# A convolution and a gated feed-forward layer on one core: the second stream's x issued first, the reciprocals' diagonal in two operations, a first weight slice of 256 columns, and shared casts

## The chip, the cores and the metric

The kernel runs on one core of a Trainium2 chip. The time is the device time of one execution in microseconds. The engines named below are TensorE (PE; its weight loads are PEld), VectorE (DVE), ScalarE (ACT), GpSimd (POOL) and SyncE (SP). DMA transfers are issued from the queues of SP and GpSimd; a transfer that converts from 32 to 16 bits is issued from GpSimd here.

## What is computed

x is (8, 4096, 192) in float32: 8 batches, 4096 positions, 192 channels in 8 heads of 24. A causal convolution over 7 positions has one set of 7 weights for each head, after a softmax over the 7. Its result, taken as 32768 tokens of 192, goes through a layer with a gate.

```
w = exp(weight - max(weight));  w = w / (sum(w) + 1e-9)        # (8, 7)
a[b, s, h, :] = sum over k of w[h, k] * x_pad[b, s + k, h, :]    # 6 zeros ahead of each batch
out = (relu(a @ w_gate) * (a @ w_val)) @ w_out                  # 192 -> 1536 -> 192
```

## The kernel before

**Streams and units.** The 8 batches are two streams of 4 (`st` 0 and 1). A unit is 1024 tokens of each stream, 16 units in all; a window is 512 tokens, two to a unit. The gate and value matmuls have only 64 rows to contract at a time (three chunks `c` of 64 channels), so the two streams lie on partitions 0 to 63 and 64 to 127 and run beside each other in the two halves of the array. That is why the gate and value weights `Wg` and `Wv` lie twice in SBUF: each slice of columns is loaded to partitions 0 to 63 by DMA (`load_w`, converting) and then copied to partitions 64 to 127 (`both_halves`; `pool_halves` does it on GpSimd for both weights).

**One unit.** `gate_val` (L528) goes through 12 slices `f` of 128 of the 1536 hidden channels. For each it makes the gate and the value product of both streams in two PSUM tiles (L541), then ACT applies the relu (`gr`, L552) and VectorE multiplies by the value product into `hT` (L553). There are four PSUM tiles of two banks, used in turn, so slice f+2 reuses the tiles of slice f. `project` multiplies `hT` by `Wo` (L570), and the result is copied and stored. The convolution of later units is done beside this on VectorE, ACT and GpSimd ("lanes"), from a transposed copy of x.

**The opening.** The first unit can't wait for the lanes, so its convolution runs on TensorE, as banded matrices. `first_block` (L388) makes the first window: for each chunk `c`, `conv_dense` (L352) multiplies pieces of x by the bands, 40 matmuls (L377) a chunk, and the result is evicted to `xc` (L392). In chunk 0 all pieces 1 to 4 of stream 0 come first, then those of stream 1, then piece 0 of both. `second_block` does the second window ahead of slice f=5.

The x of the first block comes in three transfers: stream 0, pieces 1 to 4, on SP in float32 into a staging area (`stage`, L104, in the room of the tile `prods`; issue L122), from where ACT casts it in two parts of the channels (L317); stream 1, pieces 1 to 4, on GpSimd, converted on the way (L127); piece 0 of both streams on SP into the staging area (L138), behind a clearing of its first rows (L137), cast by VectorE (L335).

**The bands.** `weight` lands in `wr`. VectorE takes the maximum (L251), ACT the exponentials into `ex`, 16 copies of each (L254); the row KW of `ex` holds 1e-9. VectorE sums (L258), takes the reciprocal (L259), and lays it on a diagonal of 8x8, `over` (L261), from the mask `spaced`, which GpSimd clears (L126) and fills with a diagonal (`affine_select`, L128). From the mask VectorE also makes `same` and `places` (L238). PE spreads the normalised weights over partitions (L272); VectorE makes `diag` (L282); 14 small matmuls (L292) place them as bands in PSUM; the bands are cast to 16 bits, heads 0 to 2 and 3 on VectorE, 4 to 7 on ACT (L329). The taps for the lanes are scaled on ACT (L304) and copied over partitions by DMAs on SP (L310). Between these steps PE runs matmuls on constants whose results nobody reads (`warm_up`, L154): 6 of 512 columns and one of 256 ahead of the spread matmul, 512 behind it, and 512 behind L292.

**Order.** The kernel is written with a manual schedule: each engine does its instructions in the order of the program, and waits are set from the data. GpSimd's order in the opening is: clear `spaced`, stream 1's x, the mask, weight slices 0, 1, 2 (each gate, then value), the x of the second block, slice 3, `pool_halves(2)`, slice 4, the gate half of slice 5, `pool_halves(3)`, the value half of slice 5. The slices' borders (`CUTS`, L165) are 0, 128, 384, 640, 896, 1152, 1536. VectorE copies slice 0 to the upper half while chunk 0 is computed (L358), and slice 1 after the first block and ahead of the first `hT` product (L659). After that come `pool_halves(4)`, `Wo`, `pool_halves(5)` and the first lane on GpSimd.

## Time and profile before

| | us |
|---|---|
| median of 3 runs | 765.97 (765.93 to 766.0) |
| profiled execution, span from first to last instruction | 764.4 |
| around the span (median less span) | 1.6 |
| PE busy | 760.3 (99%) |
| VectorE busy | 705.6 (92%) |
| ACT busy | 600.9 (79%) |
| GpSimd busy | 378.4 (50%) |
| first gate matmul (L541) on the chain | 7.72 |

The profiled execution has no time of its own beside its span, so it is set against the median of the runs. Times on a timeline count from the first instruction. PE's matmuls are pipelined: one of 512 columns is shown with 0.376 us, while the next pair starts after 0.216 us. A line such as L154 is a line of the kernel before; the changed kernel has other numbers for the same lines. The idle time in brackets is put down to what came last before the instruction started.

### The profile page before, as it was taken

To read this page: it belongs to the slowest core of one execution; us is meant where nothing else is said; L and a number is where in the kernel's file an instruction comes from. 1 tells how busy PE (TensorE), PEld (TensorE's weight loads), DVE (VectorE), ACT (ScalarE), POOL (GpSimd) and SP (SyncE) were. 2 spreads that over 40 slices of the span, in tenths; PEclk is the share of its full clock that TensorE was granted. 3 is DMA by queue.
4 is the path that set the end of the run, shared out by engine and by line. 5 is a ranking of instruction groups with operands and counts; after the bars stand their busy time and mean duration, and the time that the engine had idled before them with its cause. 6 is when DMAs were issued, how large, how long until landed. Compare 5 with 4: busy or idle time off the path is not lost.

```text
span 764.4 us, 25103 instructions
## 1 busy us (share of the span) xinstructions
PE 760.3 (99%) x10929; PEld 501.3 (66%) x10929; DVE 705.6 (92%) x763; ACT 600.9 (79%) x735; POOL 378.4 (50%) x244
## 2 busy tenths in 40 slices
PE   9999999999999999999999999999999999999998
PEld 5494674947649476584855848567494674947648
DVE  7998999999999999999999999999999999999891
ACT  6787887878878887887878878787787887876571
POOL 9419448093571926729175390853909347090000
PEclk9999999999999999999999999999999999999999
DMA  9969039290452805528073271722819134220202
GB/s 123 134 102 148 7 96 81 65 111 22 95 67 83 97 23 107 49 85 94 30 112 40 85 94 44 120 16 90 89 44 125 13 97 60 66 48 15 71 1 84
DMA packets 131830, 56.00 MB, mean 73 GB/s; under 512 B 96392, under 2 KB 131720, under 8 KB 131720
## 3 DMA queue, kind: packets, MB, share of 16 engines
q1 hardware_dynamic: 90680, 38.81, 23.9%
q0 software_dynamic: 40896, 15.50, 20.3%
q8 instruction: 85, 1.39, 0.8%
q14 instruction: 25, 0.20, 0.1%
q10 hardware_dynamic: 144, 0.10, 0.0%
HBM read 31.48 MB, written 25.17 MB: 74 GB/s over the span
## 4 chain that ended last, share of the span: by engine, by line
PE 99%; DVE 0%; ACT 0%; issue 0%
PE ps L541 65%; PE ps L570 32%; PE ps L619 1%; PE ps L377 0%; PE ps L154 0%; PE ps L411 0%; DVE band L329 0%; PE ps L272 0%; ACT acc L596 0%; PE ps L292 0%
## 5 line engine op out<-in xcount | busy, mean ns | idle before, releaser
L553 DVE TENSOR_TENSOR hT<-gr,ps 128x1024 f16<-128x1024 f16 (+1 forms) x386 | 469.0, 1216 | 36.6 <-ACT gr L552 9.4
L552 ACT ACTIVATE gr<-ps 128x1024 f16<-128x1024 f32 (+1 forms) x386 | 392.9, 1019 | 101.9 <-PE ps L541 99.7
L491 POOL TENSOR_TENSOR prods<-prods 128x1344 f32<-128x1344 f32 x70 | 212.4, 3034 | 290.0 <-DVE prods L487 286.7
L541 PE MATMUL ps<-xc,Wg 64*128 64x512 f16 x2304 | 311.9, 376 | 0.0
L541 PE MATMUL ps<-xc,Wv 64*128 64x512 f16 x2304 | 311.9, 376 | 0.0
L570 PEld LDWEIGHTS <-hT 64*128 64x128 f16 x5952 | 245.9, 94 | 3.7
L570 PE MATMUL ps<-Wo,hT 64*128 64x192 f16 x5952 | 248.1, 243 | 0.0
L541 PEld LDWEIGHTS <-Wv 64*128 64x128 f16 x2304 | 129.8, 94 | 118.5 <-DVE hT L553 0.3
L541 PEld LDWEIGHTS <-Wg 64*128 64x128 f16 x2304 | 112.3, 94 | 132.8 <-issue 0.2
L515 DVE SCALAR_TENSOR_TENSOR acc<-x_r,tap,acc 128x576 f32<-128x576 f16 x225 | 165.3, 813 | 0.0
L485 ACT ACTIVATE prods<-x_r,tap 128x448 f32<-128x448 f16 x222 | 130.1, 660 | 0.0
L596 ACT COPY out_s<-ps 128x768 f32<-128x768 f32 (+1 forms) x64 | 45.5, 711 | 51.3 <-PE ps L570 40.0
L203 POOL DMA_DIRECT2D x_e<-in_x_dram x58 | 47.0, 823 | 16.6 <-ACT acc L501 12.8
L465 POOL COPY x_p<-x_e 128x960 f16<-128x960 f16 (+1 forms) x58 | 50.3, 906 | 1.2 <-DMA x_e<-in_x_dram 1.1
L491 POOL TENSOR_TENSOR xc<-prods 128x1344 f16<-128x1344 f32 x14 | 42.4, 3029 | 1.1
L515 DVE SCALAR_TENSOR_TENSOR xc<-x_r,tap,acc 128x576 f16<-128x576 f16 x45 | 34.1, 813 | 0.0
L501 ACT ACTIVATE acc<-x_r,tap 128x576 f32<-128x576 f16 x45 | 31.4, 763 | 0.0
L487 DVE TENSOR_SCALAR prods<-x_r,tap 128x448 f32<-128x448 f16 x70 | 26.6, 450 | 0.0
L596 DVE COPY out_s<-ps 128x384 f32<-128x384 f32 (+1 forms) x16 | 8.7, 541 | 11.9 <-PE ps L619 9.4
L619 PE MATMUL ps<-Wo,hT 128*128 128x192 f16 x96 | 8.1, 246 | 0.0
L619 PEld LDWEIGHTS <-hT 128*128 128x128 f16 x96 | 7.9, 98 | 0.2 <-issue 0.2
L154 PE MATMUL ps<-const-bfloat16-1.0 128*128 128x512 bf16 (+1 forms) x9 | 3.9, 572 | 0.8 <-PEq L719 0.8
(54 smaller groups left out, 56.3 us busy)
## 6 DMA issues: line engine op xcount, KB each, us to landing
out_dram<-out_s SPq DMA_DIRECT2D x62, 384.0 KB, 2.7
x_e<-in_x_dram POOLq DMA_DIRECT2D x34, 192.0 KB, 7.4
x_e<-in_x_dram POOLq DMA_DIRECT2D x24, 240.0 KB, 5.6
x_r<-x_p SPq DMA_TRANSPOSE x131, 5.1
Wo<-in_moe_w_out_dram POOLq DMA_DIRECT2D x1, 576.0 KB, 7.3
x_h<-in_x_dram POOLq DMA_DIRECT2D x2, 210.0 KB, 4.8
Wg<-in_moe_w_gate_dram POOLq DMA_DIRECT2D x4, 96.0 KB, 4.1
Wv<-in_moe_w_val_dram POOLq DMA_DIRECT2D x4, 96.0 KB, 4.0
```

What stands on the lines that cost most here:

```text
L203: first = nc.gpsimd.dma_start(out=xe[:, j0 + start : j0 + n, st, :, :].rearrange("p j c r -> p j (c r)"), in_=bass.AP(tensor=x.tensor, off ...
L465: nc.gpsimd.tensor_copy(out=xp[:, j0 : j0 + n, :, st, :], in_=xe[:, j0 : j0 + n, st, :, :])
L485: engine.activation(out=out, in_=in_, func=ACTF.Copy, scale=scale)
L487: engine.tensor_scalar(out=out, in0=in_, scalar1=scale, scalar2=None, op0=ALU.mult)
L491: nc.gpsimd.tensor_tensor(out=pr[:, 0] if k < KW - 1 else xc[v + 1][:, :, LDVE:UNIT], in0=pr[:, 0], in1=pr[:, k], op=ALU.add,)
L501: nc.scalar.activation(out=accs[v][:, c, :], in_=shifted(v, c, 0, 0), func=ACTF.Copy, scale=tap[:, c, 0:1],)
L515: nc.vector.scalar_tensor_tensor(out=xc[v][:, c, 0:LDVE] if k == KW - 1 else acc[:, c, :], in0=shifted(v, c, k, 0), scalar=tap[:, c, k : k ...
L541: nc.tensor.matmul(out=pss[i][:, st, :], lhsT=W[64 * st : 64 * st + 64, c, 128 * f : 128 * (f + 1)], rhs=xcb[64 * st : 64 * st + 64, c, WI ...
L552: nc.scalar.activation(out=gr[:, sts], in_=pss[0][:, sts], func=ACTF.Relu)
L553: nc.vector.tensor_tensor(out=h[:, f, sts], in0=gr[:, sts], in1=pss[1][:, sts], op=ALU.mult)
L570: mm = nc.tensor.matmul(out=outs[q], lhsT=h[64 * r : 64 * r + 64, f, st, 128 * q : 128 * (q + 1)], rhs=Wo[64 * r : 64 * r + 64, f, :], sta ...
L596: one(out=dst[:, step * j : step * j + step], in_=src[:, step * j : step * j + step])
```

## The change

Seven places change, all in the opening:

- GpSimd issues stream 1's x ahead of the clearing of `spaced` and of the mask.
- The staging area's first rows are cleared by GpSimd, behind the mask, instead of VectorE.
- The first warm-up is 5 of 512 and one of 384 columns; the last one 512 and 256.
- The weight slices have 256 columns each. Slice 0 now covers f=0 and f=1. VectorE copies its first 128 columns to the upper half during chunk 0, and the other 128 after the first block, ahead of slice 1.
- Slice 1's gate and value loads are two calls, and between them GpSimd casts part of stream 0's x: pieces 3 and 4, channels 64 and up. ACT casts the first 64 channels of all pieces, and of pieces 1 and 2 the rest.
- The diagonal `over` is made without `sm`: a row of `ex` gets 2^127 off the diagonal and 0 on it, the sum over the rows is taken for each column, and its reciprocal is 1/sum on the diagonal and next to 0 off it. `sm` and the taps are made later, on VectorE, ahead of the band casts.
- In the first block VectorE evicts chunk 2 instead of chunk 1.

```diff
     nc.sync.dma_start(out=stage(0, SUB, 0, 1, 1, GSUB - 1), in_=body(0))
+    nc.gpsimd.dma_start(out=xts[0][0:SUB, 1:GSUB, 1, :], in_=body(1))
     ones = const.tile([128, SUB], FP)
...
     nc.gpsimd.memset(spaced[:], 0.0)
-    nc.gpsimd.dma_start(out=xts[0][0:SUB, 1:GSUB, 1, :], in_=body(1))
     nc.gpsimd.affine_select(
...
-    nc.vector.memset(stage(0, 32, 0, 2, 0, 1), 0.0)
+    nc.gpsimd.memset(stage(0, 32, 0, 2, 0, 1), 0.0)
...
-    warm_up(512, 512, 512, 512, 512, 512, 256)
+    warm_up(512, 512, 512, 512, 512, 384)
...
-    CUTS = [0, 128, 384, 640, 896, 1152, DFF]
+    CUTS = [0, 256, 512, 768, 1024, 1280, DFF]
...
-    def both_halves(copy, s, dst):
-        cols = slice(CUTS[s], CUTS[s + 1])
+    def both_halves(copy, s, dst, half=None):
+        lo, hi = CUTS[s], CUTS[s + 1]
+        cols = slice(lo, hi) if half is None else slice(lo + 128 * half, lo + 128 * half + 128)
         copy(out=dst[64:128, :, cols], in_=dst[0:64, :, cols])
...
+    def cast_x(copy, j0, j1, cols):
+        copy(
+            out=xts[0][0:ROWS0, j0:j1, 0, cols],
+            in_=stage(0, ROWS0, 0, 1, j0, j1 - j0)[:, :, cols],
+        )
+
     load_w(0)
-    load_w(1)
+    load_w(1, 1)
+    cast_x(nc.gpsimd.tensor_copy, 3, 5, slice(64, D))
+    load_w(1, 2)
     load_w(2)
...
+    FAR = 2.0**127
+    nc.vector.tensor_scalar(
+        out=ex[:, KW + 1, 0:H],
+        in0=spaced[0:H, 0, GAP : GAP + H],
+        scalar1=-FAR,
+        scalar2=FAR,
+        op0=ALU.mult,
+        op1=ALU.add,
+    )
...
-    nc.vector.tensor_reduce(out=sm[:], in_=ex[:, :, 0], axis=mybir.AxisListType.X, op=ALU.add)
-    nc.vector.reciprocal(sm[:], sm[:])
     over = const.tile([H, H], FP)
-    nc.vector.tensor_scalar(
+    nc.vector.tensor_reduce(
         out=over[:],
-        in0=spaced[0:H, 0, GAP : GAP + H],
-        scalar1=sm[:],
-        scalar2=None,
-        op0=ALU.mult,
-    )
+        in_=ex[:, :, 0:H].rearrange("h k j -> h j k"),
+        axis=mybir.AxisListType.X,
+        op=ALU.add,
+    )
+    nc.vector.reciprocal(over[:], over[:])
...
-    warm_up(512)
+    warm_up(512, 256)
 
     taps = const.tile([H, KW], FP)
-    nc.scalar.activation(taps[:], ex[:, 0:KW, 0], ACTF.Copy, scale=sm[:])
+    sm = const.tile([H, 1], FP)
+    nc.vector.tensor_reduce(
+        out=sm[:], in_=ex[:, 0 : KW + 1, 0], axis=mybir.AxisListType.X, op=ALU.add
+    )
+    nc.vector.reciprocal(sm[:], sm[:])
+    nc.vector.tensor_scalar(
+        out=taps[:], in0=ex[:, 0:KW, 0], scalar1=sm[:], scalar2=None, op0=ALU.mult
+    )
...
-    for cols in (slice(0, 64), slice(64, D)):
-        nc.scalar.copy(
-            out=xts[0][0:ROWS0, 1:GSUB, 0, cols],
-            in_=stage(0, ROWS0, 0, 1, 1, GSUB - 1)[:, :, cols],
-        )
+    cast_x(nc.scalar.copy, 1, 5, slice(0, 64))
+    cast_x(nc.scalar.copy, 1, 3, slice(64, D))
...
-            both_halves(nc.vector.tensor_copy, 0, Wg)
-            both_halves(nc.vector.tensor_copy, 0, Wv)
+            both_halves(nc.vector.tensor_copy, 0, Wg, 0)
+            both_halves(nc.vector.tensor_copy, 0, Wv, 0)
...
-            copy = nc.vector.tensor_copy if c == 1 else nc.scalar.copy
+            copy = nc.vector.tensor_copy if c == 2 else nc.scalar.copy
...
     first_block()
+    both_halves(nc.vector.tensor_copy, 0, Wg, 1)
+    both_halves(nc.vector.tensor_copy, 0, Wv, 1)
     both_halves(nc.vector.tensor_copy, 1, Wg)
     both_halves(nc.vector.tensor_copy, 1, Wv)
```

More of the change, by code (lines that the diff above doesn't have):

```diff
@@ L230 @@
     load_w(5, 2)
-    ex = const.tile([H, KW + 1, SEG], FP)
+    ex = const.tile([H, KW + 2, SEG], FP)
     nc.vector.memset(ex[:], 1e-9)
@@ L256 @@
     )
-    sm = const.tile([H, 1], FP)
-    nc.vector.tensor_reduce(out=sm[:], in_=ex[:, :, 0], axis=mybir.AxisListType.X, op=ALU.add)
-    nc.vector.reciprocal(sm[:], sm[:])
     over = const.tile([H, H], FP)
-    nc.vector.tensor_scalar(
+    nc.vector.tensor_reduce(
         out=over[:],
-        in0=spaced[0:H, 0, GAP : GAP + H],
-        scalar1=sm[:],
-        scalar2=None,
-        op0=ALU.mult,
+        in_=ex[:, :, 0:H].rearrange("h k j -> h j k"),
+        axis=mybir.AxisListType.X,
+        op=ALU.add,
     )
+    nc.vector.reciprocal(over[:], over[:])
     same = const.tile([SUB, SEG], FP)
```

## The prediction

> **What bounds the kernel now.** I read the page's head and its chain of waits in order of time first, then the timeline of the opening, then the DMA issues of the same stretch. The page's head:
>
> ```profile
> span 764.4 us, 25103 instructions
> ```
>
> The chain in order of time (start, length, what):
>
> ```profile
> 0.85 2.93 PE ps L154 x7
> 3.78 0.47 PE ps L272 x2
> ...
> 4.79 0.27 PE ps L292 x7
> ...
> 5.09 0.52 DVE band L329
> ...
> 5.65 2.08 PE ps L377 x106
> 7.72 6.66 PE ps L541 x60
> ...
> 57.46 31.08 PE ps L541 x288
> ```
>
> TensorE is the bound from end to end. Once the gate/value matmuls (L541) start at about 7.7 us, the work ahead of it is a fixed list; the change touches no matmul of it. So the time can move in two ways only: the start of L541 moves, or PE is made to stand still later. A stand-still shows against the steady pace, 31.08/288 = 0.108 us a matmul, or 1.295 us for the twelve of one slice f. The profiled span is 764.4 us against a median of 765.97 us, so some 1.6 us lie around the span; I take that as constant, and put every difference onto 765.97. Half a microsecond is 0.07% here; 0.2%, about what a measurement of this kernel can tell from no change, is 1.53 us.
>
> The opening on the timeline (start, length, engine, line, what, count; in brackets the idle time before and who ended it):
>
> ```profile
> 0.81 0.33 POOL L126 MEMSET spaced<- 112x280 f32 x1 [0.29 <-POOLq L719]
> ...
> 1.07 0.38 DVE L137 MEMSET prods<- 32x384 f32 x1
> ...
> 1.42 0.88 POOL L127 DMA_DIRECT2D x_h<-in_x_dram  x1 [0.28 <-issue]
> ...
> 1.67 0.48 SPq L138 DMA_DIRECT2D prods<-in_x_dram  x1
> ...
> 2.39 0.36 POOL L128 TENSOR_SCALAR_AFFINE_SELECT spaced<-ones 112x112 f32<-112x112 f32 x1
> ...
> 2.67 0.68 POOL L170 DMA_DIRECT2D Wg<-in_moe_w_gate_dram  x1
> 2.79 0.15 DVE L258 TENSOR_REDUCE sm<-ex 8x1 f32<-8x8 f32 x1 [0.45 <-ACT ex L254]
> ...
> 3.25 0.22 DVE L261 TENSOR_SCALAR over<-spaced,sm 8x8 f32<-8x8 f32 x1
> ...
> 3.66 0.42 DVE L238 TENSOR_REDUCE places<-spaced 112x22 f16<-112x154 f32 x1
> ...
> 4.29 0.29 DVE L282 TENSOR_TENSOR diag<-ps,same 112x128 f16<-112x128 f32 x1 [0.20 <-PE ps L272]
> ...
> 5.09 0.51 DVE L329 CAST band<-ps 128x336 f16<-128x336 f32 x1 [0.51 <-PE ps L292]
> ...
> 5.12 0.92 ACT L317 CAST x_h<-prods 110x256 f16<-110x256 f32 x2 [1.60 <-DMA prods<-in_x_dram]
> ...
> 5.67 0.36 DVE L335 CAST x_h<-prods 102x384 f16<-102x384 f32 x1
> ...
> 5.95 0.27 DVE L329 CAST band<-ps 128x112 f16<-128x112 f32 x1
> ...
> 6.18 1.38 PEld L377 LDWEIGHTS <-x_h 110*32 110x32 f16 x104 [0.15 <-DMA x_h<-in_x_dram]
> ...
> 6.49 0.28 DVE L177 COPY Wg<-Wg 64x384 f16<-64x384 f16 x1 [0.27 <-DMA Wg<-in_moe_w_gate_dram]
> 6.75 0.58 DVE L177 COPY Wv<-Wv 64x384 f16<-64x384 f16 x1
> ...
> 7.36 0.69 DVE L392 CAST xc<-ps 128x512 f16<-128x512 f32 x1
> ...
> 7.93 0.58 ACT L392 CAST xc<-ps 128x512 f16<-128x512 f32 x1 [0.49 <-PE ps L377]
> ...
> 8.08 0.42 DVE L177 COPY Wg<-Wg 64x768 f16<-64x768 f16 x1
> ...
> 8.43 0.53 DVE L177 COPY Wv<-Wv 64x768 f16<-64x768 f16 x1
> ...
> 9.38 0.82 POOL L177 COPY Wg<-Wg 64x768 f16<-64x768 f16 x1
> ...
> 9.62 1.28 DVE L553 TENSOR_TENSOR hT<-gr,ps 128x512 f16<-128x512 f16 x2 [0.67 <-ACT gr L552]
> ...
> 10.96 0.33 PEld L541 LDWEIGHTS <-Wv 64*128 64x128 f16 x6 [0.34 <-DVE hT L553]
> 10.97 0.82 PE L541 MATMUL ps<-xc,Wv 64*128 64x512 f16 x6
> ...
> 42.22 3.19 POOL L203 DMA_DIRECT2D x_e<-in_x_dram  x4 [12.75 <-ACT acc L501]
> ```
>
> Two places decide. First, the convolution starts at 5.65 because three things end together: the band cast (5.09 + 0.51), the cast of the first stream's x behind its DMA (5.12), and right after them the second stream's x, for which PE's weight loads wait at 6.18. Second, the value matmuls of slice f=2 start at 10.97 just after the two hT products of f=0 end (9.62 + 1.28 = 10.90): they reuse the PSUM banks which those products read. VectorE had only 0.67 us of idle time ahead of these products.
>
> The DMA issues of the opening (KB, us from issue to landing):
>
> ```profile
> x_h<-in_x_dram POOLq DMA_DIRECT2D x1, 168.0 KB, 4.7
> prods<-in_x_dram SPq DMA_DIRECT2D x1, 144.0 KB, 4.0
> ...
> Wg<-in_moe_w_gate_dram POOLq DMA_DIRECT2D x1, 48.0 KB, 3.8
> ...
> Wv<-in_moe_w_val_dram POOLq DMA_DIRECT2D x1, 96.0 KB, 3.3
> ```
>
> Two stretches of the opening (bounds and length; busy time of PE, PEld, DVE, ACT, POOL; granted clock, DMA share, GB/s):
>
> ```profile
> 3.20:3.80 0.60, 0.60 (x3) 0.09 (x1) 0.55 (x3) 0.30 (x1) 0.60 (x2) 1.00 1.08 367
> ...
> 5.10:5.60 0.50, 0.37 (x7) 0.08 (x4) 0.50 (x1) 0.48 (x2) 0.50 (x2) 1.00 1.66 178
> ```
>
> **The change, part by part.**
>
> *GpSimd's queue.* The second stream's x issues at 0.81 instead of 1.42 (0.88 long, to 1.69); then the clearing of `spaced` (0.33, to 2.02), the mask (0.09 gap and 0.36, to 2.47, against 2.75 now), and the clearing of the first block's head, which leaves VectorE (0.38 there, I take 0.4: to 2.9). A DMA issue behind a clearing came 0.28 later (row of 1.42), so the first weight slice issues at 3.15 instead of 2.67: 0.48 later. x of the second stream landed at 1.42 + 4.7 = 6.12; it lands between 5.51 (all of the 0.61 kept) and 6.12 (the DMA rings are full anyway); I take 5.8. That removes PE's wait at 6.18, worth up to 0.2 us.
>
> *The head of the first block on SP.* Its DMA waited for VectorE's clearing (1.07 + 0.38) and issued at 1.67; now it waits for GpSimd's, at 2.9, and issues near 3.0. Behind it on SP are only the tap copies, which nothing in these 11 us reads. It landed at 1.67 + 4.0 = 5.67, exactly when L335 began. It queued behind 336 KB, so 1.33 us of later issue need not be 1.33 us of later landing: bounds 5.67 and 7.0, I take 6.0, nearer to the low end because the ring was busy until about 5. L335 (0.36) and the band of head 3 (0.27) then end at 6.6 instead of 6.22, where the second chunk of the convolution needs it (24 matmuls after 6.18 at 1.54/104 us each: about 6.55): 0.1 us of PE, bounds 0 and 1.0.
>
> *The reciprocals.* Reduce, reciprocal and scaling ran from 2.79 to 3.47. Reduce (now 8x72, between the 0.15 row and 0.4) and reciprocal remain: to about 3.25, 0.2 us sooner. The far-value operation sits in the idle time before 2.79 (0.45), 0.22 long as L261, if the mask is there by 2.47. The warm-up loses 384 of 3,328 columns of its 2.93 us: 0.34 us, so the spread matmul (3.78) can start near 3.45. The two reductions behind (to 3.66 + 0.42 = 4.08) end near 3.85, and diag (4.29) starts near 4.05. But the taps' reduce, reciprocal and scaling, now on VectorE between diag and the band cast, cost what the three cost before, 0.68 us, in a gap of 0.51: 4.35 + 0.68 = 5.03 against 5.09. The band gains 0.06 us, bounds 0 and 0.3. The longer second warm-up (256 columns, 0.11 us at the steady pace) lies in PE's wait for the band.
>
> *The casts.* The first one still waits for x of the first stream, which landed at about 5.1. Earlier traffic of the second stream can only take bandwidth from it: bounds 0 and +0.61 (the whole head start), I take +0.1. So the convolution still starts at 5.65 to 5.75. Sharing shortens ACT's second cast; GpSimd's cast has 256 elements a lane, against 768 in 0.82 us at 9.38: between 0.27 and 0.82, I take 0.45, from 5.15 to 5.6, before the second chunk wants it at 6.55. It blocks GpSimd's queue: the value half of slice 1 issues at 5.9 (0.28 behind the cast), where it came right behind the gate half.
>
> So L541's start moves by -0.2 (no wait for x) +0.1 (first x) +0.1 (head of block): I take -0.05, bounds -0.25 and +0.4.
>
> At the first x the transfers' sharing is the question: the rate fell from 367 to 178 GB/s once the second stream's converting transfer was the one running. The Trainium skill, DMA: Bandwidth & Descriptors, on arbitration, says that each DMA engine alternates between the queues that have work, packet by packet. By that rule a head start of 0.6 us delays the first x by about half of it, 0.3 us, and my term would be +0.3 in place of +0.1.
>
> *The wider first slice.* A 96 KB slice landed as soon as 3.3 us after its issue, a 48 KB one in 3.8 (2.67 + 3.8 = 6.47): Wg at 3.15 + 3.3 = 6.45 and, one issue (0.68) later, Wv at 7.13. The half copies (0.28, and 0.58 for Wv) then end near 7.7; the first value matmul comes some 0.22 (two paces) after 7.72. Hidden by 0.2 us; bound +0.4 if the ring delays them.
>
> *The evictions.* ACT takes chunk 1 behind chunk 0 and ends about when VectorE did (8.05). VectorE takes chunk 2, at 7.93, for 0.69 instead of 0.58: 8.62, +0.1 on PE, swallowed by the next term.
>
> *VectorE before the hT products.* This is where I see the cost. Before: chunk 1 at 7.36, copies of slice 1 to 8.96, 0.67 idle, hT at 9.62. Now: chunk 2 from 7.93 (7.88 with the shift) to 8.57, then four copies, two of 384 columns (0.28 each, 0.58 at worst) and two of 768 (0.42, 0.53). With the 0.08 by which neighbours overlap they take 1.28 to 1.57, and the first hT starts at 9.9 to 10.2; I take 10.07. That is 0.45 us after 9.62, and the second ends 0.45 later, so f=2's value matmuls start 0.45 later than 10.97, because they started 0.07 after it already. PE has no slack to win this back. The value half of slice 1 lands at 5.9 + 3.3 = 9.2, ahead of its copy at about 9.5; if GpSimd's cast takes longer this adds up to 0.3. GpSimd runs some 1.5 us later from here; its later slices are wanted one f (1.295 us) later each, and its idle 12.75 us before 42.22 takes up the rest: no cost. If that cover failed, PE would wait at a slice's first matmul by what is missing, 0.2 us as a bound.
>
> Sum: the second place overrules the first, since PE waits there for VectorE: 765.97 + 0.45 = 766.42, where the -0.05 is already in. Low end of the terms: start -0.25 and copies at 1.28: +0.0; high end: +0.4, 1.57 and the late load: +1.3.
>
> **The rivals.**
>
> *A: the VectorE wait*, as above: 766.1 to 767.0, 766.4.
>
> *B, faster: the opening shortens and VectorE keeps up.* x of both streams lands early, the start of L541 moves by -0.3 (0.34 of warm-up columns is the most the mask path gives), and the copies run faster than their rows. It decides if the four copies are through by about 9.4. For: 0.67 us of idle time is there. Against: the added work, two copies and a later eviction (7.36 to 7.93), is about 1.1 us. It gives 765.6.
>
> *C: the input transfers.* First x or the block's head lands 0.4 us or more later, since the second stream's transfer now runs beside them, so L541 starts 0.3 to 0.5 late and the VectorE wait comes on top: 766.8 to 767.3. For: the landing at 5.67 had no slack. Against: the same bytes cross the same rings.
>
> *D: PE stays slow longer.* The warm-up rows show 0.45 us per 512 columns (2.93 for 6.5 of them), the steady rows 0.216, and L292 at 4.79 runs about at the turn. If the shorter warm-up put the turn off by as long again (3.9 us from 0.85), the work between 4.8 and 8.7 ran at half pace: up to 1.9 us, less 0.2 us of idle time there: 767.7. Against: other matmuls fill the place of the 384 columns. The Trainium skill, TensorE: Matmul & The Clock Gate, Part 1, says that the full clock is granted after about 3.4 us of sustained work, in a window that runs freely. The turn near 4.8 agrees with that; by that rule a gap of 0.2 us does not lose it, while a window missed would give this rival's price.
>
> *E: nothing moves*: all terms cancel within 0.1 us: 766.0.
>
> **How the numbers follow.** A 0.62, B 0.18, C 0.10, D 0.04, E 0.06. The predicted time is A's, 766.4. The range runs from B's 765.6 to 767.2, which leaves out D and the last of C and B. Faster by over 0.2% (under 764.4) would need more than the whole of the opening's waits: 0.01. Slower by over 0.2% (over 767.5) is D and C's far end: 0.05. The rest, 0.94, is within.
>
> **What would show it.** In the changed profile: the band cast still near 5.0; the first x cast at 5.1 to 5.3; no wait of PE's weight loads for the second stream's x; L541 within 0.2 us of 7.72; four L177 copies on VectorE behind its eviction of chunk 2, and no idle time before the first hT, at about 10.1; f=2's value matmuls near 11.4. The step is wrong if the first hT still waits for ACT's gr, or if f=2's value matmuls follow f=2's gate matmuls without a gap. The prediction as a whole is wrong if PE stands still after 20 us, where I see nothing that the change reaches.

## The result, and the profile after

The changed kernel took 769.46 us (median of 5 runs, 767.63 to 769.65) against 766.0 us (765.93 to 766.02): 1.004 times the time before, with an interval of 1.0027 to 1.0052. It is slower by 3.46 us; the forecast was 766.4, with a range up to 767.2, and a chance of 0.05 for slower.

The profiled execution took 769.46 us. The page's head of the changed kernel:

```profile
span 767.4 us, 25109 instructions
```

The span grew by 3.0 us. 769.46 - 767.4 = 2.06 us lie around it, where the prediction held 1.6 us constant; that part is taken up with the experiments (the span of every run is known, and in 137 runs of the kernel before 1.65 to 1.79 us lie around it, 1.72 in the middle).

The chain of waits of the changed kernel, in order of time (start, length, what):

```profile
1.38 0.10 POOL x_h L123
...
2.25 0.37 POOL spaced L127
2.68 0.33 POOL spaced L128
3.03 0.37 DVE ex L264
...
3.79 0.20 DVE over L282
4.12 0.51 PE ps L287 x2
...
12.21 0.40 DVE Wv L178
...
13.25 0.69 DVE hT L572
14.07 3.42 PE ps L560 x30
...
60.56 31.08 PE ps L560 x288
```

Before, the chain began with PE's warm-up. Now GpSimd's x issue, clearing and mask set the spread matmul (L287), and VectorE's copies and `hT` products set the value matmuls at 14.07. From there nothing is lost: those 288 matmuls take 31.08 us as before, and start 3.10 us later (60.56 against 57.46).

Before's timeline of PE, rows that the prediction did not need (start, length, engine, line, what, count):

```profile
4.63 0.62 PE L292 MATMUL ps<-diag,places 112*128 112x64 f16 x14
...
5.65 2.08 PE L377 MATMUL ps<-band,x_h 110*32 110x104 f16 x120 [0.18 <-DVE band L329]
7.66 0.39 PE L541 MATMUL ps<-xc,Wg 64*128 64x512 f16 x2
7.88 0.38 PE L541 MATMUL ps<-xc,Wv 64*128 64x512 f16 x2
```

The opening of the changed kernel on its timeline:

```profile
1.38 0.88 POOL L123 DMA_DIRECT2D x_h<-in_x_dram  x1 [0.86 <-POOLq L740]
...
2.96 0.41 POOL L137 MEMSET prods<- 32x384 f32 x1
3.03 0.35 DVE L264 TENSOR_SCALAR ex<-spaced 8x8 f32<-8x8 f32 x1 [0.70 <-POOL spaced L128]
...
3.39 0.31 SPq L138 DMA_DIRECT2D prods<-in_x_dram  x1
...
4.12 0.51 PE L287 MATMUL ps<-over,ex 8*112 8x8 f32 x2 [0.67 <-DVE over L282]
4.53 0.71 ACT L223 CAST x_h<-prods 110x256 f16<-110x256 f32 x2 [1.78 <-DMA prods<-in_x_dram]
...
5.01 0.90 PE L307 MATMUL ps<-diag,places 112*128 112x64 f16 x14
...
5.73 0.83 PE L154 MATMUL ps<-const-bfloat16-1.0 128*128 128x512 bf16 x2
6.49 3.08 PE L396 MATMUL ps<-band,x_h 110*32 110x104 f16 x120
...
9.50 0.61 PE L560 MATMUL ps<-xc,Wg 64*128 64x512 f16 x2
...
9.90 0.64 PE L560 MATMUL ps<-xc,Wv 64*128 64x512 f16 x2
10.32 0.50 PE L560 MATMUL ps<-xc,Wg 64*128 64x512 f16 x2
10.33 0.28 DVE L178 COPY Wg<-Wg 64x384 f16<-64x384 f16 x1
10.40 0.84 POOL L178 COPY Wg<-Wg 64x768 f16<-64x768 f16 x1
...
10.54 0.84 DVE L178 COPY Wv<-Wv 64x384 f16<-64x384 f16 x1
10.66 0.38 PE L560 MATMUL ps<-xc,Wv 64*128 64x512 f16 x2
...
11.30 0.98 DVE L178 COPY Wg<-Wg 64x768 f16<-64x768 f16 x1
...
12.21 0.40 DVE L178 COPY Wv<-Wv 64x768 f16<-64x768 f16 x1
...
14.07 0.82 PE L560 MATMUL ps<-xc,Wv 64*128 64x512 f16 x6 [0.66 <-DVE hT L572]
```

Three things are to be seen. First, PE's pace: 14 small matmuls took 0.62 us before and 0.90 us now; the convolution's 120 took 2.08 us and now 3.08; the first gate and value pairs follow each other after 0.22 us before (7.66, 7.88), and now after 0.40, 0.42, 0.34 (9.50, 9.90, 10.32, 10.66). PE reached its full pace (called the turn below) at about 10.5 us, not 4.8. Second, PE stands idle for 0.67 us ahead of the spread matmul. Third, the two copies of VectorE that start while GpSimd copies (10.54 and 11.30) take two to three times as long as the other two: 0.84 against 0.28 for 384 columns, 0.98 against 0.40 for 768.

The granted clock does not show the first of these. The window of the convolution (bounds, length; busy time of PE, PEld, DVE, ACT, POOL; granted clock, DMA share, GB/s):

```profile
6.49:9.50 3.01, 3.01 (x122) 2.85 (x122) 1.15 (x4) 1.23 (x3) 3.01 (x5) 1.00 1.16 131
```

It says 1.00 in the slow stretch too; the pace has to be read from the durations.

Where the 3.10 us at f=2's value matmuls (14.07 against 10.97) come from, by these rows:

| | us |
|---|---|
| the convolution starts later: 6.49 against 5.65 | +0.84 |
| it lasts longer up to the first gate matmul: 3.01 (to 9.50) against 2.01 (to 7.66) | +1.00 |
| from there to f=2's value matmuls: 4.57 against 3.31 | +1.26 |

All of the last part is the wait for VectorE. The three slow pairs in it (0.18 + 0.20 + 0.12 us over 0.22 each) add nothing to it, since f=2's value matmuls wait for `hT` and `hT` waits for VectorE's copies; they only fill part of PE's wait. In e1 below all pairs run at full pace, and the same stretch takes 4.58 us (8.94 to 13.52), with 1.10 us of idle time instead of 0.66.

### The profile page after: what moved, and what is told of

Same layout as the page of the kernel before. It is cut to its first block, busy times and chain, and to the rows that moved or that the text cites. A ratio compares the mean times of both kernels' runs of the same rounds, so it can differ in the third digit from the quotient of the medians.

```text
span 767.4 us, 25109 instructions
## 1 busy us (share of the span) xinstructions
PE 762.3 (99%) x10929; PEld 515.3 (67%) x10929; DVE 707.1 (92%) x767; ACT 600.5 (78%) x734; POOL 378.6 (49%) x246
## 3 DMA queue, kind: packets, MB, share of 16 engines
q8 instruction: 85, 1.39, 0.8%
## 4 chain that ended last, share of the span: by engine, by line
PE 98%; DVE 1%; issue 0%; POOL 0%; ACT 0%; DVEq 0%; POOLq 0%
PE ps L560 64%; PE ps L589 32%; PE ps L638 1%; PE ps L396 1%; PE ps L154 0%; DVE Wv L178 0%; PE ps L430 0%; DVE hT L572 0%; PE ps L307 0%; DVE xc L411 0%; PE ps L287 0%; DVE Wg L178 0%; POOL spaced L127 0%; DVE ex L264 0%; POOL spaced L128 0%
## 5 line engine op out<-in xcount | busy, mean ns | idle before, releaser
L560 PEld LDWEIGHTS <-Wv 64*128 64x128 f16 x2304 | 134.0, 94 | 115.7 <-issue 1.4
L560 PEld LDWEIGHTS <-Wg 64*128 64x128 f16 x2304 | 120.6, 94 | 124.4 <-issue 0.6
L396 PEld LDWEIGHTS <-x_h 110*32 110x32 f16 (+7 forms) x240 | 4.2, 107 | 1.0 <-issue 1.0
```

What stands on the lines that cost most here:

```text
L560: nc.tensor.matmul(out=pss[i][:, st, :], lhsT=W[64 * st : 64 * st + 64, c, 128 * f : 128 * (f + 1)], rhs=xcb[64 * st : 64 * st + 64, c, WI ...
```

## The experiments

Two theories stood at the start. One: the changed order on GpSimd makes the mask late, the idle time ahead of the spread matmul that comes of it keeps PE slow. The rival: the shortened warm-up itself keeps PE slow. Beside both, VectorE's copies. In each diff "before" or "changed" says which kernel is edited. The kernel before ran beside all of them, at 765.97 to 766.04 us in the middle.

### The order on GpSimd, and the diagonal

e1, changed: GpSimd's x issue goes back behind the clearing.

```diff
-    nc.gpsimd.dma_start(out=xts[0][0:SUB, 1:GSUB, 1, :], in_=body(1))
...
     nc.gpsimd.memset(spaced[:], 0.0)
+    nc.gpsimd.dma_start(out=xts[0][0:SUB, 1:GSUB, 1, :], in_=body(1))
```

> The changed kernel with one part undone: GpSimd clears the mask's tile ahead of the second stream's x, as before. Theory 1 (the early issue gains nothing, it holds the mask back, PE idles ahead of the spread matmul and so turns to full pace some 5.8 us late): mask done near 2.75 instead of 3.0, spread matmul near 3.5, full pace from about 4.8, L541 starts at 7.4 to 7.9, and only the VectorE wait ahead of f=2 is left: 766.0 to 766.6. Theory 2 (the shorter warm-up alone loses the turn): full pace still after 8 us, 768 or more.

Measured: 769.37 us (768.92 to 769.37), 1.004 (1.0027 to 1.0052): nothing won. Its timeline:

```profile
2.79 0.35 DVE L264 TENSOR_SCALAR ex<-spaced 8x8 f32<-8x8 f32 x1 [0.47 <-POOL spaced L128]
...
3.87 0.51 PE L287 MATMUL ps<-over,ex 8*112 8x8 f32 x2 [0.42 <-DVE over L282]
...
7.22 0.36 DVE L354 CAST x_h<-prods 102x384 f16<-102x384 f32 x1 [1.38 <-DMA prods<-in_x_dram]
...
13.52 0.82 PE L560 MATMUL ps<-xc,Wv 64*128 64x512 f16 x6 [1.10 <-DVE hT L572]
```

The mask came 0.24 us earlier and so did the spread matmul; PE still idled 0.42 us, reached its full pace between 7.4 and 7.6, and the convolution stood waiting for the block's head, cast at 7.22, until 7.64. The theory that the order alone does it falls.

e2, before: the same x issue moved to the front, nothing else.

```diff
+    nc.gpsimd.dma_start(out=xts[0][0:SUB, 1:GSUB, 1, :], in_=body(1))
     ones = const.tile([128, SUB], FP)
...
-    nc.gpsimd.dma_start(out=xts[0][0:SUB, 1:GSUB, 1, :], in_=body(1))
```

> The kernel before with one part done alone: the second stream's x issued ahead of the clearing of the mask's tile. Theory 1: the issue starts no earlier than 1.35, the mask ends 0.25 to 0.3 later, the spread matmul comes some 0.4 later and PE idles between 3.6 and 4.1; if that idle time alone loses the turn, 768 to 769.5; if the longer warm-up still saves it, 766.2 to 766.6. Theory 2: 766.0 to 766.4.

Measured: 765.92 us (765.85 to 767.77), 1.0001 (0.9992 to 1.001). The part costs and wins nothing, and its first row says why:

```profile
1.39 0.88 POOL L123 DMA_DIRECT2D x_h<-in_x_dram  x1 [0.88 <-POOLq L719]
```

With nothing ahead of it the issue starts at 1.39, against 1.42 behind the clearing. The clearing had been free. In this trace the convolution takes 1.75 us against 2.08, without the wait at 6.18 for the second stream's x that the prediction priced at up to 0.2 us. One trace does not settle that price: the convolution of e9, without the edit, takes 1.74, and that of e11, with it, 2.10.

e9, before: only the new diagonal, with the sum and the taps on VectorE.

```diff
+    nc.vector.tensor_scalar(out=ex[:, KW + 1, 0:H], in0=spaced[0:H, 0, GAP : GAP + H], ...
-    nc.vector.tensor_scalar(out=over[:], ... scalar1=sm[:], ...
+    nc.vector.tensor_reduce(out=over[:], in_=ex[:, :, 0:H].rearrange("h k j -> h j k"), ...
+    nc.vector.reciprocal(over[:], over[:])
...
-    nc.scalar.activation(taps[:], ex[:, 0:KW, 0], ACTF.Copy, scale=sm[:])
+    nc.vector.tensor_scalar(out=taps[:], in0=ex[:, 0:KW, 0], scalar1=sm[:], ...
```

> The kernel before with the diagonal in two operations and the taps on VectorE, all else as before (mask at 2.75, long warm-up). By the prediction's term the band gains 0.06 us: 765.9 to 766.0. By the traces since: the far-value operation (0.35 us in e1) has to wait for the mask and stands between the exponentials and the sum, so the spread matmul comes at 3.87 instead of 3.71 and the band at 5.3 to 5.4: 766.2 to 766.4.

Measured: 766.12 us (765.84 to 768.11), 1.0002 (0.9993 to 1.001). Its timeline:

```profile
2.79 0.16 DVE L255 TENSOR_SCALAR ex<-spaced 8x8 f32<-8x8 f32 x1 [0.46 <-POOL spaced L128]
...
5.03 0.51 DVE L342 CAST band<-ps 128x336 f16<-128x336 f32 x1
...
7.65 0.78 DVE L177 COPY Wg<-Wg 64x768 f16<-64x768 f16 x1
```

The band cast comes at 5.03, the figure of the prediction, but not by its path: `diag` is made at 4.29 as before (4.05 was forecast), and the 14 small matmuls, at full pace from their start at 4.63, took 0.57 us instead of 0.62. The span of the profiled run is 763.9 us, 0.5 below that of before, but 2.05 us lie around it.

e18, before: only the taps' scaling moves from ACT to VectorE.

```diff
-    nc.scalar.activation(taps[:], ex[:, 0:KW, 0], ACTF.Copy, scale=sm[:])
+    nc.vector.tensor_scalar(out=taps[:], in0=ex[:, 0:KW, 0], scalar1=sm[:], scalar2=None, op0=ALU.mult)
```

> The kernel before with the taps' scaling on VectorE instead of ACT, nothing else. If it is the taps' move that adds 0.3 us outside the span: time less span 2.0. If it is the diagonal (far value, reduce and reciprocal): 1.6 to 1.75. Median 765.9 to 766.3 either way.

Measured: 766.24 us (766.0 to 766.71), 0.9999 (0.9989 to 1.0009). In its 10 runs 1.97 to 2.06 us lie around the span; in every kernel here that has the taps on VectorE it is 1.97 to 2.08, in every one that has them on ACT 1.65 to 1.79, without overlap. So this one move adds 0.3 us outside the span, and that is 0.3 of the 3.46 us. Which part of the time around the span grows, the trace does not say.

### The warm-up

e3, changed: the first warm-up is made longer than before's.

```diff
-    warm_up(512, 512, 512, 512, 512, 384)
+    warm_up(512, 512, 512, 512, 512, 512, 512, 256)
```

> The changed kernel with a longer first warm-up (seven of 512 and one of 256 columns), so that PE works until the spread matmul at 4.1. If idle time of PE costs the turn: full pace from about 4.8, the convolution back to 2.1 us, 766.8 to 767.6, what is left being the later start of the convolution (0.8) and the VectorE wait. If the loss is something else: 769 as the changed kernel.

Measured: 767.50 us (766.9 to 769.29), 1.0023 (1.0013 to 1.0033): 1.96 us of the 3.46 are back. PE on its timeline:

```profile
0.85 3.10 PE L154 MATMUL ps<-const-bfloat16-1.0 128*128 128x512 bf16 x8 [0.85 <-PEq L740]
4.13 0.33 PE L287 MATMUL ps<-over,ex 8*112 8x8 f32 x2 [0.18 <-DVE over L282]
...
4.84 0.57 PE L307 MATMUL ps<-diag,places 112*128 112x64 f16 x14
...
7.08 1.36 PE L396 MATMUL ps<-band,x_h 102*32 102x96 f16 x88 [0.54 <-DVE x_h L354]
```

The spread matmul is as late as in the changed kernel (4.13 against 4.12), but it takes 0.33 us instead of 0.51, and the 14 small matmuls take 0.57: PE is at full pace already. The turn lies within the first warm-up, whose 3,840 columns took 3.10 us; in e7, where the turn came at about 4.6, the same columns took 3.36. What remains is a wait of 0.54 us in the middle of the convolution, for the head of the first block.

e5, before: only the warm-up is shortened as in the change.

```diff
-    warm_up(512, 512, 512, 512, 512, 512, 256)
+    warm_up(512, 512, 512, 512, 512, 384)
```

> The kernel before with the first warm-up shortened to five of 512 and one of 384 columns, nothing else. The scaled diagonal is ready at 3.47 there, so PE idles only some 0.2 us ahead of the spread matmul. If the length of PE's idle time decides about the turn to full pace (0.83 us idle in the changed kernel, 0.62 in e1): turn near 4.8 to 5.4, 765.8 to 766.2. If the 384 columns themselves decide: turn after 6 us, 767 to 768.5.

Measured: 766.49 us (765.89 to 767.62), 1.0002 (0.9994 to 1.0011). By the interval that is no difference, but the runs fall apart: 5 of 11 spans are 764.2 to 764.3 us, the others 764.8 to 765.9. The profiled one is of the others:

```profile
4.49 0.90 PE L292 MATMUL ps<-diag,places 112*128 112x64 f16 x14
...
5.75 2.35 PE L377 MATMUL ps<-band,x_h 110*32 110x104 f16 x120
```

The small matmuls are slow to the end (0.90), and the full pace comes at about 7.0. The time lies between the two that were expected.

e12, before: `warm_up(512, 512, 512)`, so that PE idles far longer ahead of the spread matmul than in the changed kernel.

> The kernel before with a first warm-up of three matmuls of 512 columns only, so that PE idles from 2.1 to 3.6 ahead of the spread matmul, and nothing else. If PE's idle time ahead of the spread matmul sets how late the turn to full pace comes: turn after 7 us in nearly all runs, 767.3 to 768.5. If not: 765.9 to 766.1.

Measured: 766.73 us (766.5 to 767.59), 1.0009 (1.0 to 1.0017), less than the 767.3 to 768.5 expected.

```profile
3.61 0.51 PE L272 MATMUL ps<-over,ex 8*112 8x8 f32 x2 [1.32 <-ACT taps L304]
...
5.76 2.35 PE L377 MATMUL ps<-band,x_h 110*32 110x104 f16 x120
```

PE idled 1.32 us, twice as long as in the changed kernel, and yet the convolution runs as in e5. So the idle time does not set by its length when the full pace comes.

e11 and e14, before: x first as in e2; in e11 the last piece of the first warm-up is 64 columns instead of 256, in e14 the last warm-up is `warm_up(512, 256)`.

> e2 (kernel before with the second stream's x first, 765.92) with 192 columns less in the first warm-up, so that the spread matmul follows the diagonal at once. A candidate for a faster version: if the turn to full pace holds, everything up to the convolution comes 0.1 to 0.15 us sooner, 765.75 to 765.85. If the turn comes later as in e5: 766.2 to 767.

> e2 (kernel before, second stream's x first) with 256 more warm-up columns behind the small matmuls, where PE waits for the band. A candidate for a faster version, and a test whether more work of PE there brings the turn forward: 765.75 to 765.95 with fewer runs at 766.2 and above than e2 (3 of 11). If the work ahead of the spread matmul alone decides: as e2, 765.92 with the same spread of runs.

Measured: e11 765.94 us (765.7 to 767.64), 1.0008 (0.9999 to 1.0017); e14 766.02 us (765.91 to 766.3), 0.9997 (0.9988 to 1.0006). Neither beats the kernel before. But the spans tell more than the medians: those of e11 are 764.0 to 764.2 us in 6 runs and 765.6 to 765.9 in 5, those of e14 764.2 to 764.6 in all 11. Of 137 spans of the kernel before, 125 are 764.0 to 765.0 us and 12 are 765.8 to 766.5; the middles of the two groups are 1.8 us apart there, and 1.5 in e11. A run seems to draw an early or a late turn, and the shorter the warm-up, the likelier the late one: 12 in 137 in before, 5 in 11 in e11, and in e5 3 in 11 at 765.6 to 765.9 with 3 more in between, at 764.8 to 765.2. It is not that simple throughout: e12, with the shortest, has none below 764.8 and 9 of 11 at 764.8 to 765.2. Each kernel has the trace of one run, so that the upper spans are late turns is argued from their distance and not shown.

### The head of the first block

e7, changed: the long warm-up of e3, and the head's first rows cleared by VectorE again. e16: the changed kernel with that clearing alone.

```diff
-    nc.gpsimd.memset(stage(0, 32, 0, 2, 0, 1), 0.0)
+    nc.vector.memset(stage(0, 32, 0, 2, 0, 1), 0.0)
```

> As e3 (changed kernel, long warm-up), and the first rows of the staging area cleared by VectorE as before, so that the block's head is issued at about 1.7 instead of 3.4. In e3 PE waited 0.75 us inside the convolution for it (landed 6.4). If that is what it costs: the head lands at 5.4 to 5.7, no wait inside the convolution, L541 at 7.6 to 7.8, 766.5 to 766.9 against 767.5 (767.27 in the profiled run) of e3. If the first x lands later in return (5.0 instead of 4.5): 766.9 to 767.3.

> The changed kernel with the staging area's first rows cleared by VectorE as before, so that the block's head lands near 5.5 instead of 6.4. If the idle time inside the convolution is what puts the turn off: 767.4 to 768.4. If the idle time of 0.83 us ahead of the spread matmul does it alone: 769.0 to 769.5.

Measured: e7 766.89 us (766.49 to 767.22), 1.0008 (1.0 to 1.0017); e16 768.09 us (768.01 to 769.31), 1.0032 (1.0021 to 1.0044), within the 767.4 to 768.4 expected. In e7 the wait of 0.54 us is gone, and so is 0.61 us of e3's time. (The 0.75 us in the text for e7 is VectorE's wait for the head; PE's is 0.54.) In e16 the win by the medians is larger, 1.37 us: in the changed kernel the far-value operation took 0.35 us beside GpSimd's clearing (2.96 to 3.37), in e16 it takes 0.16; the spread matmul starts at 3.93 instead of 4.12, and the full pace comes at about 7.75 instead of 10.5. That the clearing moves the turn is not shown by this: the changed kernel's convolution shows no idle time inside it (120 matmuls in one row), and the turn differs as much between kernels with the same work ahead of it (e6 and e13 below).

e16 and e7 differ in the first warm-up alone, as the changed kernel and e3 do. The long one wins 1.20 us here, and the spans of the two do not meet: 766.0 to 767.3 us in the 7 runs of e16, 764.5 to 765.2 in the 11 of e7.

e15, changed: the old diagonal and taps. e17: e15 and the clearing on VectorE.

```diff
-    nc.vector.tensor_scalar(out=ex[:, KW + 1, 0:H], in0=spaced[0:H, 0, GAP : GAP + H], ...
-    nc.vector.tensor_reduce(out=over[:], in_=ex[:, :, 0:H].rearrange("h k j -> h j k"), ...
-    nc.vector.reciprocal(over[:], over[:])
+    nc.vector.tensor_reduce(out=sm[:], in_=ex[:, :, 0], ...
+    nc.vector.reciprocal(sm[:], sm[:])
+    nc.vector.tensor_scalar(out=over[:], in0=spaced[0:H, 0, GAP : GAP + H], scalar1=sm[:], ...
```

> The changed kernel with the old diagonal and the old taps. If the far-value operation behind the late mask is what holds the spread matmul until 4.12: spread matmul at 3.5 to 3.65, the band near 5.1, the turn 1 to 3 us sooner, 767.6 to 768.6. If the late mask alone holds it: spread still after 3.9 and 769.0 to 769.6.

> e15 (changed kernel with the old diagonal and taps) with the clearing on VectorE too: PE idles 0.3 us ahead of the spread matmul and no longer inside the convolution. If unbroken work of PE from about 3.6 on is what brings the turn: turn near 7 as in e5, 766.6 to 767.6 (e5's 766.49 and some of the slices' cost). If not: 768.5 or more.

Measured: e15 769.14 us (767.21 to 769.64), 1.0031 (1.002 to 1.0043); e17 768.34 us (767.74 to 768.9), 1.003 (1.002 to 1.004), more than the 766.6 to 767.6 expected. PE in e15:

```profile
3.58 0.51 PE L281 MATMUL ps<-over,ex 8*112 8x8 f32 x2
...
9.40 0.61 PE L547 MATMUL ps<-xc,Wg 64*128 64x512 f16 x2
```

These two went against the theory that the gap ahead of the spread matmul decides. e15 starts it at 3.58, with a gap of 0.12 us, and PE is slow nearly as long as in the changed kernel (to about 9.8, the pair at 9.40 still taking 0.61 us); e17 starts it at 3.76, with a gap of 0.30, and is at full pace at about 8.4. All 9 kernels with a first warm-up of 2,944 columns or fewer turned late in their trace, between 7.0 and 10.5 us, and the 11 with 3,136 or more between 3.4 and 6.5. What picks the moment within either group stays open, and it isn't PE's work ahead of it alone: before, e4, e8, e9 and e18 run the same matmuls up to 4.63 us, and the 14 small ones that follow took 0.62, 0.91, 0.86, 0.57 and 0.90 us, with turns from 4.4 (e9) to 6.5 (e4).

### The slices and VectorE's copies

e4, before: slices of 256 columns, the four copies, the eviction of chunk 2. e8: e4 with GpSimd's first copies one load later.

```diff
-    CUTS = [0, 128, 384, 640, 896, 1152, DFF]
+    CUTS = [0, 256, 512, 768, 1024, 1280, DFF]
...
+    both_halves(nc.vector.tensor_copy, 0, Wg, 1)
+    both_halves(nc.vector.tensor_copy, 0, Wv, 1)
...
-            copy = nc.vector.tensor_copy if c == 1 else nc.scalar.copy
+            copy = nc.vector.tensor_copy if c == 2 else nc.scalar.copy
```

```diff
-    pool_halves(2)
     load_w(4)
+    pool_halves(2)
```

> The kernel before with the 256-column slices, the four copies on VectorE and the eviction of chunk 2 on VectorE, nothing else. By the VectorE term of the prediction, f=2's value matmuls start 0.45 us late: 766.4 (766.1 to 766.8). If VectorE keeps up: 766.0.

> As e4 (slices alone on the kernel before), with GpSimd's copies of slice 2 behind the loads of slice 4 instead of ahead of them, so that they no longer run beside VectorE's copies of slice 1. In e4 VectorE's last copy took 0.98 us beside GpSimd's copies, where the same copy took 0.53 before. If the two engines' copies hold each other up: that copy takes 0.4 to 0.55, the first hT starts at 10.0 to 10.1 instead of 10.5, 766.4 to 766.7 against 767.04. If they don't: 767.0.

Measured: e4 767.04 us (766.19 to 767.05), 1.0007 (0.9998 to 1.0016); e8 766.23 us (765.95 to 767.95), 1.0001 (0.9992 to 1.001). e4's copies:

```profile
9.38 0.82 POOL L178 COPY Wg<-Wg 64x768 f16<-64x768 f16 x1
9.50 0.98 DVE L178 COPY Wv<-Wv 64x768 f16<-64x768 f16 x1
...
11.95 0.82 PE L542 MATMUL ps<-xc,Wv 64*128 64x512 f16 x6 [0.65 <-DVE hT L554]
```

Here the wait of PE for VectorE that the prediction forecast stands by itself: 0.65 us. From the first gate matmul to f=2's value matmuls it is 4.11 us in e4 (7.84 to 11.95) against 3.31 before: +0.80. The copy at 9.50 took 0.98 us beside GpSimd's. In e8 GpSimd's copies begin at 10.61, and VectorE's last one, at 9.49, takes 0.40; the same stretch is 3.76 us (7.59 to 11.35). So the slices with their copies cost +0.45 us there, the figure of the prediction, and the collision 0.35 more. By the medians it is 1.00 us in e4, more than expected, and 0.19 in e8, less than expected and within the noise.

e13, changed: the same swap as in e8. e6, changed: the old slices, copies and eviction. e10: e6 with e7's two edits.

> The changed kernel with GpSimd's copies of slice 2 behind the loads of slice 4, as e8 did for the slices alone. In the changed kernel VectorE's copies of 0.84 and 0.98 us run beside GpSimd's copies at 10.4 to 12.0. If the two hold each other up: copies of 0.27 and 0.45, the first hT 0.8 to 1.1 us sooner, 768.4 to 768.9. If PE's slow start covers it: 769.3 to 769.6.

> The changed kernel with the old slices, copies and evictions back (slice 0 of 128 columns, chunk 1 on VectorE), the rest as changed. If the VectorE wait ahead of f=2 is a cost of its own of about 1 us, as e4 (767.04 against 765.97) says: 768.0 to 768.7, and no wait of PE for the hT products. If the late turn swallows it: 769.2 to 769.6.

> As e7 (changed kernel, long warm-up, block's head cleared by VectorE) with the old slices and evictions too. Left of the change: the second stream's x first, the shared casts, the diagonal and the taps. If the late mask and the diagonal cost 0.3 to 0.4 and nothing else is left: 766.1 to 766.5. If the parts named so far do not hold the whole loss: 766.8 or more.

Measured: e13 768.26 us (767.6 to 769.77), 1.0029 (1.0018 to 1.004); e6 768.01 us (767.4 to 768.73), 1.0022 (1.0013 to 1.0031); e10 766.81 us (766.14 to 767.14), 1.0007 (0.9998 to 1.0016). VectorE in e13, where GpSimd's copies begin at 11.70:

```profile
9.61 0.28 DVE L178 COPY Wg<-Wg 64x384 f16<-64x384 f16 x1
...
10.01 0.40 DVE L178 COPY Wg<-Wg 64x768 f16<-64x768 f16 x1
10.33 0.40 DVE L178 COPY Wv<-Wv 64x768 f16<-64x768 f16 x1
```

Apart, the four take 1.12 us from first start to last end (9.61 to 10.73); in the changed kernel they took 2.28 (10.33 to 12.61). The same copies are 0.28 and 0.40 alone, 0.84 and 0.98 beside GpSimd's. The Trainium skill, Advanced Engine Details and Errata, on VectorE's performance modes, says that VectorE's second SBUF port is shared with GpSimd, and that the two block each other there. The rows agree; here it costs 0.56 to 0.58 us a copy. It does not explain e9's copy of 0.78 us at 7.65, beside which GpSimd only issued DMAs. The stretch from the first gate matmul to f=2's value matmuls is 3.43 us in e13 (8.77 to 12.20) and 3.26 in e6 (8.93 to 12.19). In the changed kernel it is 4.57: the collision costs 1.14 us there, about the 1.16 by which the four copies grew (2.28 against 1.12), and the slices without it 0.17. The medians move by 1.20 in e13 and 1.45 in e6, but in both traces PE is also at full pace earlier, at about 7.8 and 8.2. PE in e6:

```profile
6.49 2.50 PE L396 MATMUL ps<-band,x_h 110*32 110x104 f16 x120
```

The changed kernel's convolution starts at 6.49 too, after the same PE rows, and takes 3.08 us. Neither edit changes what PE does before that, so a turn that comes over 2 us earlier is a draw of the run and not the work of the edit, and with 5 to 11 runs the medians hold some of that luck.

### The parts together

Undone one after the other, by medians: changed 769.46; with the long warm-up (e3) 767.50; with the head cleared by VectorE (e7) 766.89; with the old slices (e10) 766.81; before 766.0. That is 1.96 for the warm-up, 0.61 for the head and 0.89 for the slices and all the rest; e10 lies at 766.8, above the 766.1 to 766.5 that would have left no unnamed part. The last cannot be divided by medians, because e10's spans fall into two groups, 764.1 to 764.3 us (5 runs, as in before) and 764.8 to 765.1 (6 runs). Of it 0.3 lies outside the span (e18), and by the traces the slices are worth 0.47: the stretch from the first gate matmul to f=2's value matmuls is 3.73 us in e7 (7.70 to 11.43) and 3.26 in e10 (7.48 to 10.74). In another order the parts come out otherwise: with the short warm-up the head is 1.37 (e16) and the slices 1.45 (e6), and the warm-up is 1.20 once the head is mended (e16 to e7). With the short warm-up the turn varies from run to run by more than these differences, so they are not shown to be the parts' own.

## Why the prediction was wrong

**The step that failed** is the one against rival D, "other matmuls fill the place of the 384 columns". Two things in it were wrong. The columns were taken away ahead of the spread matmul, on the claim that it can then start near 3.45, and were put back behind the small matmuls (two warm-ups at 5.73), where they delayed the convolution, at half pace, to 6.49. And the spread matmul did not start at 3.45 but at 4.12. So PE lost columns and gained idle time. The rival had a chance of 0.04 and a price of up to 1.7 us; two pairs of kernels that differ in the first warm-up alone put a long one at 1.96 us (changed and e3) and at 1.20 (e16 and e7). Its mechanism, a later turn, was right; its chance was not. What the 384 columns cost by themselves is not shown: the long warm-ups have 3,840 columns, where before has 3,328, the changed kernel was not run with 3,328, and on the kernel before the loss of the 384 is 0.49 us by the medians, within the noise (e5). The row that told of the risk was there: L292 ran at the turn. But one trace could not tell the margin, as the 0.57 to 0.91 us for those matmuls in e4, e8, e9 and e18 show.

The prediction named the rule of the Trainium skill, TensorE: Matmul & The Clock Gate, Part 1, and drew the wrong half of it. The Trainium skill says there that the full clock comes after a busy window of about 3.4 us, that the window runs freely, and that the count of slow matmuls so varies from run to run. By that, whoever thins out the work inside the window risks the whole of it: the turn would come up to 3.4 us later, and half of that, 1.7 us, would be lost (an estimate from the Trainium skill's figure). The spans of one kernel do lie in groups 1.5 to 1.8 us apart, which agrees. The Trainium skill also gives the variation as 0.5 us; the turns at 4.4 to 6.5 us behind the same PE work, and those of the kernels with a short warm-up, at 7.0 to 10.5 us, do not agree with that. Nor does e3 agree with 3.4 us of work: its turn came within the first warm-up, less than 3.1 us after PE's first matmul. No run here shows what the window itself saw.

**GpSimd's order.** x was to issue at 0.81; it issued at 1.38. The 0.28 us of idle time behind the clearing were read as the price of a DMA issue behind a clearing; in e2, with nothing ahead of it, the issue starts at 1.39 all the same. So the mask ended at 3.00 and not at 2.47, 0.25 later than before instead of 0.28 earlier.

**The reciprocals.** The far-value operation was put into idle time, at 0.22 us "if the mask is there by 2.47". It wasn't: the operation started at 3.03, took 0.35, and everything behind it came 0.6 to 0.7 us later than forecast (`over` ready at 3.98, not 3.25). Before, the mask was wanted only by the last of the three operations, at 3.25; now it is wanted by the first. One part of the change made the mask later, another made it needed earlier. The band cast came at 5.60 against a forecast of 5.03; with the diagonal alone (e9) it came at 5.03, but by luck: `diag` was no earlier than before, and the small matmuls happened to run at full pace from the start.

**The head of the block.** It landed at 6.43 (issue 3.39, 3.0 us), within the bounds of 5.67 to 7.0 but 0.4 later than taken. The late convolution hid it in the changed kernel; once that is mended, it shows as the 0.54 us in e3.

**First x, second x, casts.** The second stream's x kept PE from nothing, as predicted. The first x did not land later but earlier: ACT's cast began at 4.53 instead of 5.12, where +0.1 was taken. The Trainium skill, DMA: Bandwidth & Descriptors, on arbitration, would have made it +0.3 by the alternation of queues (an estimate from its rule); the row went the other way. Why stays open. With the second stream's x first on the kernel before, the cast begins at 4.80 to 4.98 (e2, e11, e14), without it at 4.61 to 5.12 (before, e9 and others), so no delay shows there either. The later issue of the head's transfer (3.39) is not the reason by itself: e7 has 4.54 with the head issued at 1.66, and e15 4.85 with 3.39. GpSimd's cast took 0.41 us for 0.45 forecast. The three terms for L541's start, -0.2, +0.1 and +0.1, add up to 0.0 and not to the -0.05 taken; nothing hangs on that.

**VectorE ahead of hT.** The mechanism was right: PE waits for `hT` at f=2's value matmuls, 0.66 us. The size was off: the four copies were put at 1.28 to 1.57 us and took 2.28. The durations came from rows where GpSimd was not copying. Had the first gate matmul come at 7.7, the four copies would have been through by 10.07, as forecast, ahead of GpSimd's own copies, which came at 10.40; since PE was late, so were VectorE's copies (from 10.33), and the two met. e7 is that case: VectorE's copies end at 9.97, GpSimd's begin at 10.07, and the stretch to f=2's value matmuls is 0.42 us longer than before (3.73 against 3.31), where 0.45 was forecast. So the rest of this term is a consequence of the step that failed.

**Constant time around the span.** Held at 1.6 us; it is 1.72 before and 1.97 to 2.08 with the taps on VectorE.

**Nothing after 20 us.** Right: from 14.07 on the two traces run alike.

## What to carry to other kernels

Matmuls that only keep PE busy are worth their time until the trace shows PE at full pace with some margin, and one trace does not show that margin, because the turn varies from run to run. Columns taken from them in one place were not replaced here by columns in another. Read the pace from the durations of equal matmuls, because the granted clock here showed nothing. When one part of a change makes something later and another makes it needed earlier, cost the two together. Before using a copy's duration, look what the neighbour engine does in that row and what it will do at the new place.

## What the runs showed of the hardware

- The half pace of PE after the start ended, by the traces, at 3.4 to 6.5 us with a first warm-up of 3,136 columns or more (11 kernels), and at 7.0 to 10.5 us with one of 2,944 or 1,536 (9 kernels). The granted clock was shown as 1.00 throughout.
- The same PE work does not give the same moment: behind the same matmuls up to 4.63 us the half pace ended at 4.4 to 6.5 us in five kernels, and behind the same work up to 6.49 us at about 8.2 in e6 and 10.5 in the changed kernel.
- A kernel's spans lie in two groups: 125 runs at 764.0 to 765.0 us and 12 at 765.8 to 766.5 for the kernel before.
- GpSimd's first DMA issue started at 1.38 to 1.43 us whether a clearing stood ahead of it or not.
- A copy on VectorE of 64x768 in 16 bits took 0.40 us, and 0.98 beside GpSimd's copies; in e9 one took 0.78 us (7.65) where GpSimd was issuing DMAs and copied nothing.
- Moving one small scaling from ACT to VectorE lengthened the time around the span from 1.72 to 2.01 us (e18), in every run.
